# Moving matrix comparisons out of the attention heads of a four-layer network: 12 instead of 18 per attention, more in the second prologue, and squares one row tile behind their folds in the last product

## The chip, the cores and the metric

The kernel runs on one core of a Trainium2 chip. A core has a matrix engine (PE, with its weight loads shown as PEld), a vector engine (DVE), a scalar engine (ACT), a general engine (POOL) and a queue that only issues transfers here (SP). Each works through its own instructions in program order and waits on semaphores of the others. The metric is the device time of one execution in microseconds; the time before is the median of three runs.

## The reference

One sequence of 2048 rows of 640 passes through four layers, twice an attention and a Fourier layer:

```python
x = x + A(layernorm(x))      # 32 heads of 20, each row sees itself and the 255 before it
x = x + B(layernorm(x))      # y = Re(DFT_seq(DFT_hidden(x))), the four DFT matrices are inputs
x = x + A(layernorm(x))
x = x + B(layernorm(x))
# A: qkv = x @ wqkv; softmax(q k^T / sqrt(20) + mask) v, then @ wo
# B: a = x @ hid_re^T, b = x @ hid_im^T;  y = seq_re @ a - seq_im @ b
```

## The kernel before

The four DFT matrices are inputs, but a real DFT matrix repeats itself up to sign: rows and columns mirrored about the middle are equal or opposite. The Fourier layers use this and multiply by a quarter or less of each matrix. So that this holds for any input, the kernel also compares the matrices with themselves on the chip. It makes 180 comparisons in all (18 tiles of the hidden matrices `hr`, `hi`, 162 of the sequence matrices `kr`, `ki`), sums the squared differences, and at the end sets a flag `ok` of one word. Every engine loads it and branches: past a slow general version of the network if the symmetry holds, into it if not. With the inputs used, the branch always passes it.

One comparison is five steps (`check`, line 1462): SP issues one transfer of 214 to 228 KB into a free buffer (L1469); two folds subtract and add the mirrored parts (`differ`, L1476, one fold for some tiles); ACT squares the result with a running sum into a column of `ring` (`square`, L1480); after each eighth comparison DVE adds eight columns (L1485). The folds stand on POOL or on DVE, as the place asks. The last comparison also starts `verdict` (two small DVE operations into `sums`), and `judge` (L1509) turns `sums` into `ok`: a memset of ones on DVE, one small matmul into bank 6 of PSUM, four small DVE operations (L1517 to L1520).

The comparisons stand at four kinds of places, always taken from one list in order, so that a comparison left out at one place is made at a later one:

- In each attention's prologue (`before_heads`: layer norm, transposes, the first projections), the local function `check` starts one after most of the eight `piece` calls and ten of the sixteen `value` calls, in a pipeline of three (`check_step`): transfer first, folds on POOL and the square on ACT two or three calls later. 16 in each.
- In each attention's `heads`, 18 comparisons (`IN_HEADS`) over the first 81 of 128 steps (`CHECKED`): the transfer at the end of a step, then the two folds on POOL and the square on ACT six, seven and nine half steps later, from `self.post`.
- In each Fourier layer (`fourier`), four after each of the products 2 to 11 (`checks`, folds on DVE), then as many as are still in the shorter-lived buffers in a `while` loop, also on DVE.
- In the last product of the second Fourier layer, four for each of the first row tiles on POOL: `checks(4, n < 5, nc.gpsimd)`, fold, fold, square one after another, then the next transfer into the same buffer.

The last product runs over eight row tiles n (`order = (7, 0, 1, ... 6)`). `straight(n, j)` makes two products in PSUM (six matmuls, L1387), ACT copies one out (L1388, tile `sent`), DVE makes `dif` and `tot` and adds both to the row tile `big` (L1375), SP stores it (L1379). `turned(n - 1, ...)` stands one row tile behind: PE reverses `tot` and `dif` (L1403, two matmuls with `flip`, into banks 2 and 3 for even n - 1 and 6 and 7 for odd), and DVE adds them to the mirrored row tile. Only the last tile's `turned(7, 6)` follows the loop.

In the heads, every step makes scores in PSUM twice: once by query rows to find the row maxima (S, L676, with DVE's masked maximum, L681), once transposed for the exponentials (T, L704, ACT's L714, POOL's masks L720 and L724), then the product with v (L739); projection matmuls fill PE's gaps (L274). The row maxima of four query blocks are turned on PE and negated on ACT (tile `mt`, L692); SP then sends them with two transfers into a row of `qp` (L694), which T needs four steps later. SP's order is the order in which the program posts its transfers, and a transfer that waits holds all behind it.

Of the kernel before, what the change touches and what calls it, by code (L numbers as in the profile page):

```python
# [7 lines left out]
F32 = mybir.dt.float32  # L8
# [42 lines left out]
PRODUCTS = [(n, c) for n in ("ce", "co", "so", "se") for c in range(3)]  # L51
SIGMA, WIDE = 513, 57
SCALED, MARGIN = 2.0 ** 40, 2.0 ** 12
IN_HEADS, CHECKED = 18, 81

CHUNKS = ((0, 16, 0, 8), (0, 16, 8, 16), (16, 24, 0, 16), (24, 32, 0, 16), (0, 32, 16, 20))

# [16 lines left out]
class Net:  # L74
# [335 lines left out]
    def before_heads(self, xsrc):  # L410
# [42 lines left out]
        def pieces(sb):  # L453
            for c in range(2):
                if sb == 0:
                    prep()
                self.piece(c, sb, "q")
                if c or sb > 1:
                    check()
                if sb and state[0] < 4 * sb + 8:  # L460
                    prep()

        def value(t):
            v, xt = vst[t // 2 % 2], self.xnt(t // 4)
            rs = slice((t % 4) * P, (t % 4 + 1) * P)
            ps = []
            for hf in range(2):
                p = self.bank("v", 320)
                cs = slice(hf * 320, (hf + 1) * 320)
                self.all3(p, [((xt[:, 0, k, rs], xt[:, 1, k, rs]), (wv[k][0][:, cs], wv[k][1][:, cs]))  # L470
                              for k in range(KC)])
                ps.append(p)
            prep()
            for hf in range(2):
                dst = v[:, 4 * hf:4 * hf + 4, t % 2, 0:84].rearrange("p q (h c) -> p q h c", c=21)[:, :, :, 1:21]
                src = ps[hf].rearrange("p (q h c) -> p q h c", q=4, h=4)
# [826 lines left out]
    def fourier(self, xsrc, xdst, more):  # L1303
# [8 lines left out]
        lasting = bufs[6:]  # L1312
        waiting = deque()

        def checks(n, again=True, eng=nc.vector):
            for _ in range(n):
                if waiting:
                    work, buf = waiting.popleft()
                    work(eng)
                    if self.checks and (again or not more and any(buf is b for b in lasting)):  # L1320
                        waiting.append((self.check(buf), buf))

        for buf in bufs:
            if self.checks:
                waiting.append((self.check(buf), buf))

        def leave(n, c, b, eng):
            k = KINDS[n][1][c][1]
# [85 lines left out]
        for n, j in enumerate(order):  # L1414
            straight(n, j)
            if n:
                turned(n - 1, order[n - 1])
            if n < 6:
                checks(4, n < 5, nc.gpsimd)
            elif n == 6 and not more:  # L1420
                checks(len(waiting), False, nc.gpsimd)
                assert not self.checks
                self.judge()
            if more:
                if n > 1:
                    self.split_w(3)
# [82 lines left out]
    def judge(self):  # L1509

        nc = self.nc
        ones = self.work.tile([P, 1], F32, name="all1", tag="rc")
        nc.vector.memset(ones, 1.0)
        p = self.banks[0:1, 6, :5]
        nc.tensor.matmul(p, ones, self.sums, start=True, stop=True)
        s = self.work.tile([1, 16], F32, name="judged", tag="sm")
        nc.vector.tensor_copy(s[:, 0:5], p)  # L1517
        nc.vector.tensor_scalar(out=s[:, 5:9], in0=s[:, 1:5], scalar1=MARGIN, scalar2=s[:, 0:1], op0=OP.mult, op1=OP.is_gt)
# [174 lines left out]
```

## Time and profile before

| | |
|---|---|
| runs | 1375.52, 1375.58, 1376.85 us; median 1375.58 |
| profiled execution | 1376.7 us, its span 1374.8 us, mean granted PE clock 0.989 |
| busy, share of the span | PE 94%, PEld 72%, DVE 71%, ACT 55%, POOL 53% |
| first prologue and heads | 0 to 150, 150 to 532 us |
| partial products and first Fourier layer | 532 to 612, 612 to 687 us |
| second prologue and heads | 687 to 830, 830 to 1202 us |
| the same again, second Fourier layer | 1202 to 1282, 1282 to 1322 us |
| last product and end | 1322 to 1374.8 us |

Busy time is the time in which an engine had an instruction in work. Matmuls overlap, so a PE that is busy throughout may still not be at its peak. In rows of the timeline the columns are the start, the time, engine, line, operation and operands, and in brackets how long the engine had idled and for whom. Names such as `qp<-mt` mean output and input; a `q` after an engine's name marks its sequencer or queue.

### The profile page before, as it was taken

To read this page: it belongs to the slowest core of one execution; us is meant where nothing else is said; L and a number is where in the kernel's file an instruction comes from. 1 tells how busy PE (TensorE), PEld (TensorE's weight loads), DVE (VectorE), ACT (ScalarE), POOL (GpSimd) and SP (SyncE) were. 2 spreads that over 40 slices of the span, in tenths; PEclk is the share of its full clock that TensorE was granted. 3 is DMA by queue.
4 is the path that set the end of the run, shared out by engine and by line. 5 is a ranking of instruction groups with operands and counts; after the bars stand their busy time and mean duration, and the time that the engine had idled before them with its cause. 6 is when DMAs were issued, how large, how long until landed. Compare 5 with 4: busy or idle time off the path is not lost. (4 is left out here: it accounts for less than half of the span.)

```text
span 1374.8 us, 37392 instructions
## 1 busy us (share of the span) xinstructions
PE 1294.4 (94%) x13350; PEld 993.6 (72%) x13350; DVE 973.6 (71%) x3123; ACT 759.6 (55%) x1651; POOL 724.4 (53%) x1502
## 2 busy tenths in 40 slices
PE   6999999999998889999999999999999989989987
PEld 6899777777776677753689987777777667777344
DVE  7723788878887774767866158878878868568575
ACT  3232378777775565437323226777777755744461
POOL 4221688777876673310323238778777865723031
PEclk9999999999999999999999999999999999999999
DMA  5675577777678774527526656677777688571464
GB/s 195 207 224 170 187 207 202 216 195 213 202 217 231 207 207 138 166 79 221 200 83 214 208 169 197 194 210 202 222 192 237 198 236 232 154 230 47 151 184 163
DMA packets 174294, 261.47 MB, mean 190 GB/s; under 512 B 36306, under 2 KB 85586, under 8 KB 174100
## 3 DMA queue, kind: packets, MB, share of 16 engines
q1 hardware_dynamic: 174100, 259.00, 62.9%
q8 instruction: 108, 1.77, 0.6%
q14 instruction: 86, 0.70, 0.2%
HBM read 175.42 MB, written 82.31 MB: 187 GB/s over the span
## 5 line engine op out<-in xcount | busy, mean ns | idle before, releaser
L681 DVE CUSTOM_DVE_ANT_0 banks<-banks,mask 128x384 f32<-128x384 f32 (+2 forms) x1024 | 527.2, 557 | 121.1 <-PE banks L676 104.4
L714 ACT ACTIVATE pt<-banks 128x768 f32<-128x768 f32 (+2 forms) x512 | 394.2, 771 | 165.6 <-PE banks L704 100.2
L720 POOL TENSOR_SCALAR_AFFINE_SELECT pt<-pt 128x256 f32<-128x256 f32 x512 | 220.1, 430 | 187.2 <-ACT pt L714 162.7
L274 PE MATMUL banks<-big,wc 64*128 64x512 f32 x1920 | 273.2, 395 | 0.4 <-DVE pt L480 0.4
L704 PE MATMUL banks<-qp,kp 61*128 61x384 f32 (+2 forms) x1024 | 210.0, 380 | 32.1 <-DVE mc L681 21.5
L676 PE MATMUL banks<-kp,qp 60*128 60x384 f32 (+2 forms) x1024 | 209.1, 352 | 5.6 <-DMA kp<-qk_d 2.9
L739 PE MATMUL banks<-pt,vq 128*32 128x128 f32 x5760 | 211.4, 278 | 0.9 <-ACT pt L714 0.8
L274 PEld LDWEIGHTS banks<-big,wc 64*128 64x128 f32 x1920 | 186.9, 186 | 22.9 <-ACT x L589 1.6
L724 POOL TENSOR_SCALAR_AFFINE_SELECT pt<-pt 128x256 f32<-128x256 f32 x448 | 187.4, 418 | 0.0
L739 PEld LDWEIGHTS banks<-pt,vq 128*32 128x32 f32 x5760 | 142.2, 110 | 49.3 <-issue 35.2
L704 PEld LDWEIGHTS banks<-qp,kp 61*128 61x128 f32 x1024 | 108.4, 185 | 95.8 <-DVE mc L681 74.6
L676 PEld LDWEIGHTS banks<-kp,qp 60*128 60x128 f32 x1024 | 124.2, 187 | 32.2 <-DVE mc L681 16.1
L681 DVE DVE_READ_ACCUMULATOR2_ANT mc<- 128x1 f32 x1024 | 144.5, 141 | 0.0
L748 ACT ACTIVATE ou<-banks 128x128 f32<-128x128 f32 (+2 forms) x288 | 73.4, 266 | 58.8 <-PE banks L739 52.2
L256 PE MATMUL banks<-qp,big 128*128 128x320 f32 x576 | 98.4, 316 | 1.0 <-POOL qp L382 1.0
L228 POOL TENSOR_TENSOR c<-x,c 128x256 fp32r<-128x256 f32 x128 | 94.5, 746 | 0.0
L256 PEld LDWEIGHTS banks<-qp,big 128*128 128x128 f32 x576 | 88.3, 192 | 1.6 <-POOL qp L382 1.4
L256 PE MATMUL banks<-qp,kp 128*128 128x320 f32 x384 | 82.1, 346 | 7.0 <-ACT big L1121 4.7
L1476 POOL TENSOR_TENSOR rr<-rr 128x171 f32<-128x171 f32 (+3 forms) x86 | 56.3, 660 | 57.9 <-DMA rr<-kr 26.6
L274 PE MATMUL banks<-big,big 64*128 64x320 f32 x912 | 80.8, 313 | 0.2 <-ACT mt L692 0.2
L256 PEld LDWEIGHTS banks<-qp,kp 128*128 128x128 f32 x384 | 60.9, 188 | 20.4 <-ACT big L1121 6.7
L274 PEld LDWEIGHTS banks<-big,big 64*128 64x128 f32 x912 | 73.9, 191 | 0.4 <-ACT mt L692 0.4
(170 smaller groups left out, 1777.0 us busy)
## 6 DMA issues: line engine op xcount, KB each, us to landing
qk_d<-c SPq DMA_DIRECT2D x80, 512.0 KB
kp<-qk_d SPq DMA_DIRECT2D x384, 80.0 KB
qp<-qk_d SPq DMA_DIRECT2D x384, 80.0 KB
o_d<-ou SPq DMA_DIRECT2D x64, 256.0 KB
v_d<-pt SPq DMA_DIRECT2D x16, 768.0 KB
vq<-v_d SPq DMA_DIRECT2D x64, 192.0 KB
kp<-ki SPq DMA_DIRECT2D x38, 228.0 KB
big<-x SPq DMA_DIRECT2D x26, 320.0 KB
```

What stands on the lines that cost most here:

```text
L228: eng.tensor_tensor(out=lo[..., c], in0=src[..., c], in1=hi[..., c].bitcast(F32), op=OP.subtract)
L256: self.nc.tensor.matmul(p, x, y, start=n == 0, stop=n == last)
L274: self.nc.tensor.matmul(ps[a], x[r], y[r], start=half + i == 0, stop=half == 1 and i == n - 1, skip_group_check=True)
L676: nc.tensor.matmul(p, qp[quad % 2][b:b + 60, z, qb * P:(qb + 1) * P], kp[quad % 2][b:b + 60, z, k0 * P:(qb + 1) * P], start=True, stop=True)
L681: nc.vector.tensor_tensor_reduce(out=p, in0=p, in1=self.mask[:, 384 - n * P:], scale=1.0, scalar=NEG, op0=OP.add, op1=OP.max, accum_out=mc ...
L704: nc.tensor.matmul(self.banks[:, banks[e], :n * P], kp[quad % 2][b:b + 61, z, kb * P:(kb + 1) * P], qp[quad % 2][b:b + 61, z, kb * P:(kb + ...
L714: nc.scalar.activation(pt[quad, kb][:, 2 * z:2 * z + 2, :n * P], self.banks[:, b0:b1 + 1, :n * P], AF.Exp, scale=SCALE)
L720: nc.gpsimd.affine_select(out=t[:, :, 0:P], in_=t[:, :, 0:P], pattern=[[0, 2], [1, P]], compare_op=OP.is_ge, fill=0.0, base=0, channel_mul ...
L724: nc.gpsimd.affine_select(out=t[:, :, 256:384], in_=t[:, :, 256:384], pattern=[[0, 2], [-1, P]], compare_op=OP.is_gt, fill=0.0, base=0, ch ...
L739: nc.tensor.matmul(self.banks[32 * h:32 * h + 32, bank, :P], vq[:, 96 * (kb % 4) + 21 * h:96 * (kb % 4) + 21 * h + 32], t[:, h, (qb - kb) ...
L748: nc.scalar.activation(ou[:, dst], self.banks[:, bank, src], AF.Copy)
L1476: eng.tensor_tensor(out=t[:, lo:hi], in0=t[:, lo:hi], in1=base.broadcast_to([P, hi - lo, w]), op=op)
```

## The change

In each attention's heads 12 comparisons are made instead of 18, still over 81 steps. The second attention's prologue (not the first) starts one in six more places: the first pieces of the first two blocks and the first four value tiles. What is not made there falls to the end: the last product of the second Fourier layer makes 20 instead of 14. Both Fourier layers keep their 50 and 48 on DVE.

In the last product the squares of a row tile's four comparisons are now made in the next row tile (`spread`, list `folded`), and the transfers into their buffers follow them there. `judge` moves from row tile 6 to row tile 7, and its memset of ones to the place ahead of the loop. The diff, cut to its core:

```diff
-IN_HEADS, CHECKED = 18, 81
+IN_HEADS, CHECKED = 12, 81
...
-                if c or sb > 1:
+                if c or sb > 1 or not first:
                     check()
...
-            if 3 < t < 14:
+            if 3 < t < 14 or t < 4 and not first:
                 check()
...
+        def spread(n, again):
+            for square, buf in folded:
+                square()
+                if again:
+                    begin(buf)
+            folded.clear()
+            for _ in range(min(n, len(waiting))):
+                (one, two, square), buf = waiting.popleft()
+                one()
+                two()
+                folded.append((square, buf))
...
+        if not more:
+            self.all = self.work.tile([P, 1], F32, name="all1", tag="rc")
+            nc.vector.memset(self.all, 1.0)
...
-            if n < 6:
-                checks(4, n < 5, nc.gpsimd)
-            elif n == 6 and not more:
-                checks(len(waiting), False, nc.gpsimd)
-                assert not self.checks
-                self.judge()
+            if not more:
+                spread(4, n < 5)
+                if n == 7:
+                    assert not self.checks and not waiting and not folded
+                    self.judge()
...
-        ones = self.work.tile([P, 1], F32, name="all1", tag="rc")
-        nc.vector.memset(ones, 1.0)
         p = self.banks[0:1, 6, :5]
-        nc.tensor.matmul(p, ones, self.sums, start=True, stop=True)
+        nc.tensor.matmul(p, self.all, self.sums, start=True, stop=True)
```

What this does to the order on the engines is shown at three places. The lines of the code have shifted: after the change `straight`'s matmuls are L1409, the flips L1425, the small matmul of `judge` L1534, the transfer of a comparison L1490, its folds L1497.

PE at the end of the last product before, from the row tile n = 6 on (`wf`, `qp`, `kp`: operands of `straight`; `ou`, `rr`: tiles `tot` and `dif`; `all`, `sums`: `judge`):

```order
L1387 MATMUL banks<-wf,qp_17317 128x321 x3
L1387 MATMUL banks<-wf,kp_17316 128x321 x3
L1403 MATMUL banks<-ou_17591,flip 128x321
L1403 MATMUL banks<-rr_17590,flip 128x319
L1515 MATMUL banks<-sums,all_17775 1x5
L1387 MATMUL banks<-wf,qp_17317 128x321 x3
L1387 MATMUL banks<-wf,kp_17316 128x321 x3
L1403 MATMUL banks<-ou_17588,flip 128x321
L1403 MATMUL banks<-rr_17587,flip 128x319
L1403 MATMUL banks<-ou_17591,flip 128x321
L1403 MATMUL banks<-rr_17590,flip 128x319
```

The same place on PE after the change:

```order
L1409 MATMUL banks<-wf,qp_17293 128x321 x3
L1409 MATMUL banks<-wf,kp_17292 128x321 x3
L1425 MATMUL banks<-ou_17569,flip 128x321
L1425 MATMUL banks<-rr_17568,flip 128x319
L1409 MATMUL banks<-wf,qp_17293 128x321 x3
L1409 MATMUL banks<-wf,kp_17292 128x321 x3
L1425 MATMUL banks<-ou_17566,flip 128x321
L1425 MATMUL banks<-rr_17565,flip 128x319
L1534 MATMUL banks<-sums,all_17562 1x5
L1425 MATMUL banks<-ou_17569,flip 128x321
L1425 MATMUL banks<-rr_17568,flip 128x319
```

The small matmul of `judge` stood ahead of the last row tile's products; it now stands behind them, between the last two pairs of flips.

SP in the first heads before, around the fourteenth sending of row maxima (`rr<-kr` is a comparison's transfer, `kp` and `qp<-qk_d` load the next heads, `sm`, `o_d`, `r_d` carry results away):

```order
L758 DMA sm<-ou_104 128x1x16
L759 DMA o_d<-ou_104 128x512
L764 DMA r_d<-rc 128x16
L1469 DMA rr_107<-kr 128x456
L639 DMA kp_573<-qk_d 20x2x512 x3
L569 DMA qk_d<-c 128x2x512
L694 DMA qp_1249<-mt 2x4x128 x2
L639 DMA kp_573<-qk_d 20x2x512 x3
```

The same sending on SP after the change:

```order
L758 DMA sm<-ou_104 128x1x16
L759 DMA o_d<-ou_104 128x512
L764 DMA r_d<-rc 128x16
L639 DMA kp_573<-qk_d 20x2x512 x3
L569 DMA qk_d<-c 128x2x512
L694 DMA qp_1249<-mt 2x4x128 x2
L639 DMA kp_573<-qk_d 20x2x512 x3
L569 DMA qk_d<-c 128x2x512
L639 DMA qp_122<-qk_d 20x2x512 x3
L666 DMA vq_100<-v_d 128x384
L1490 DMA rr_107<-kr 128x456
```

The comparison's transfer stood three rows ahead of the sending; it now stands four rows behind it, and the one before it is more than ten rows ahead.

POOL in the second prologue after the change (`rs<-rs,half` is the reciprocal root for the layer norm of a row tile, L310); before, all rows of L310 stood ahead of the first fold:

```order
L310 TENSOR_TENSOR rs<-rs,half 128x1 x2
L1497 TENSOR_TENSOR ou_8917<-ou_8917 128x171
L1497 TENSOR_TENSOR ou_8917<-ou_8917 128x228
L310 TENSOR_TENSOR rs<-rs,half 128x1
L1497 TENSOR_TENSOR rr_8918<-rr_8918 128x171
L1497 TENSOR_TENSOR rr_8918<-rr_8918 128x228
L310 TENSOR_TENSOR rs<-rs,half 128x1
L1497 TENSOR_TENSOR rr_8919<-rr_8919 128x171
L1497 TENSOR_TENSOR rr_8919<-rr_8919 128x228
L1497 TENSOR_TENSOR rr_8920<-rr_8920 128x171
L1497 TENSOR_TENSOR rr_8920<-rr_8920 128x228
L310 TENSOR_TENSOR rs<-rs,half 128x1
```

The folds of the early comparisons now stand between the reciprocal roots.

More of the change, by code (lines that the diff above doesn't have):

```diff
@@ L1313, in fourier, with begin, checks @@
         waiting = deque()
-        def checks(n, again=True, eng=nc.vector):
+        folded = []
+        def begin(buf):
+            if self.checks:
+                waiting.append((self.check(buf, True), buf))
+        def checks(n, again=True):
             for _ in range(n):
                 if waiting:
[L1318 to L1321, printed above, removed]
+                    (one, two, square), buf = waiting.popleft()
+                    one(nc.vector)
+                    two(nc.vector)
+                    square()
+                    if again or not more and any(buf is b for b in lasting):
+                        begin(buf)
+        def spread(n, again):
+            for square, buf in folded:
+                square()
+                if again:
+                    begin(buf)
+            folded.clear()
+            for _ in range(min(n, len(waiting))):
+                (one, two, square), buf = waiting.popleft()
+                one()
+                two()
+                folded.append((square, buf))
         for buf in bufs:
-            if self.checks:
-                waiting.append((self.check(buf), buf))
+            begin(buf)
         def leave(n, c, b, eng):
```

## The prediction

> **What bounds the kernel now.** I read the busy time by stage first, since the four places of the change lie in stages with different limits. The columns are the stretch, its length, then busy time with the number of instructions for PE, PEld, DVE, ACT and POOL, the granted PE clock, the share of DMA and GB/s.
>
> ```profile
> 150.00:360.00 210.00, 206.01 (x2843) 157.38 (x2839) 174.00 (x651) 154.83 (x311) 163.20 (x360) 0.99 0.69 203
> 712.00:830.00 118.00, 118.00 (x815) 106.39 (x816) 56.26 (x168) 32.39 (x92) 36.92 (x59) 1.00 0.60 188
> 830.00:1050.00 220.00, 213.90 (x3012) 162.55 (x3012) 182.01 (x682) 164.65 (x331) 173.03 (x395) 1.00 0.73 206
> 1322.00:1375.00 53.00, 40.08 (x135) 26.00 (x133) 30.60 (x76) 18.60 (x59) 17.49 (x28) 0.90 0.44 154
> ```
>
> PE carries all of them. In the second prologue it is busy without a break; in the part of the heads that holds comparisons it idles 4 to 6 us of some 215; only the last product leaves it idle for 13 us. So comparisons taken out of the heads free POOL, ACT and SP, none of which is the bound, and can gain only where PE now waits behind them. The waits of PE in those two stretches (156 to 386, then 830 to 1056 us; total, times, longest) say for what:
>
> ```profile
> PE banks L704 <- DMA qp<-mt: 2.8, 2, 1.7
> ...
> PE banks L704 <- DVE mc L681: 1.9, 5, 0.6
> ...
> PE banks L704 <- DMA qp<-mt: 4.2, 4, 1.5
> ```
>
> The largest wait is for the row maxima that SP sends late. The longest case, in the order of ACT, SP and PE, with the granted clock behind it:
>
> ```profile
> 286.25 0.25 ACT L692 ACTIVATE mt<-banks 16x128 fp32r<-16x128 f32 x1
> ...
> 287.96 0.33 SPq L1469 DMA_DIRECT2D rr<-kr  x1
> 288.49 1.18 SPq L639 DMA_DIRECT2D kp<-qk_d  x3
> 290.07 0.39 SPq L569 DMA_DIRECT2D qk_d<-c  x1
> 290.57 1.48 SPq L694 DMA_DIRECT2D qp<-mt  x2
> ...
> 294.93 0.45 PE L704 MATMUL banks<-qp,kp 61*128 61x384 f32 x2 [1.68 <-DMA qp<-mt]
> ...
> 295.00:299.00 4.00, 4.00 (x33) 3.01 (x33) 2.28 (x8) 2.14 (x4) 1.22 (x4) 0.60 0.88 253
> ```
>
> The maxima are ready at 286.25 and their first transfer starts at 290.57, 4.3 us later, because SP's row ahead of them is not yet worked off; a comparison's transfer is in that row.
>
> **The heads.** Twelve comparisons go, six from each attention. On POOL and ACT I cost them at nothing: of the 18 comparisons in 156 to 386 us (16 with `kr`, two with `hi`) the folds held up other work in two waits. Who waited for the folds there (total, times), the cost of a transfer on SP (ns, least, median, most), and what other transfers waited on SP for a comparison's transfer:
>
> ```profile
> ACT pt L714: 0.8, 1
> PEld banks L739: 0.2, 1
> ...
> L1469 SPq DMA_DIRECT2D rr<-kr x16: 333/414/822, 187.2 to 375.5; - x16
> ...
> SPq L639 <- DMA rr<-kr: 3.1, 3, 1.7
> SPq L758 <- DMA rr<-kr: 2.5, 2, 1.2
> ```
>
> What covers them is PE's own work of 98% of the stretch; were PE not the bound, the gain would be at most 1.0 us in each heads (0.8 + 0.2).
>
> On SP a comparison costs between 0.41 us (its own issue) and 0.72 us (with the waits for its landing, (3.1 + 2.5) / 18 = 0.31). Not the number counts but where the transfer stands ahead of a sending. By the order, at the fourteenth sending of each heads (here at 290.57) and the twenty-second, the last comparison ahead moves from 3 or 4 rows to 10 or more, out of the row that SP works off; at the eighteenth it comes nearer, from 10 rows to 3. The waits at these, beside the one shown:
>
> ```profile
> 383.97 0.45 PE L704 MATMUL banks<-qp,kp 61*128 61x384 f32 x2 [1.17 <-DMA qp<-mt]
> ...
> 968.32 0.45 PE L704 MATMUL banks<-qp,kp 61*128 61x384 f32 x2 [0.80 <-DMA qp<-mt]
> ...
> 1012.76 0.44 PE L704 MATMUL banks<-qp,kp 61*128 61x384 f32 x2 [1.46 <-DMA qp<-mt]
> ```
>
> Three waits shorten (1.68, 1.17, 0.80) and one lengthens (1.46); the same sending of the first heads has no wait yet and may get one, taken as half. With 0.41 us each that is -3 x 0.41 + 1.5 x 0.41 = -0.6 us. I take the lower price, because SP's next wait for a landing is as likely to be for another transfer. Bounds: all 7.0 us (2.8 + 4.2) vanish; or the three stay and two new ones of the longest kind come, +3.4 (2 x 1.68).
>
> The clock: behind the wait of 1.68 us the granted clock is 0.60 over 4 us, so 4 x 0.40 = 1.6 us of PE's work was lost. With 0.41 us taken off, that wait would be 1.27 us; the one of 1.46 us lies in a stretch whose granted clock is 1.00 (830 to 1050), so a wait of that size need not cost it. I count the half, -0.8. The Trainium skill, "TensorE: Matmul & The Clock Gate", section "What's actually happening", says that the array falls to half clock after an idle window of about 3.4 us; by it a wait of 1.68 us should have cost no clock, and the sum would be 0.8 us less of a gain. The trace differs here: the clock did fall.
>
> **The second prologue.** Six comparisons more. On PE nothing: ahead of each square ACT waits for PE anyway, and POOL waits for DVE between two reciprocal roots.
>
> ```profile
> 715.45 0.60 ACT L243 ACTIVATE c<-banks 128x512 fp32r<-128x512 f32 x1 [3.14 <-PE banks L256]
> ...
> 718.14 0.81 POOL L310 TENSOR_TENSOR rs<-rs,half 128x1 f32<-128x1 f32 x1 [3.98 <-DVE rs L307]
> ...
> L1476 POOL TENSOR_TENSOR rr<-rr x18: 507/634/958, 742.0 to 786.2; 128x171 f32<-128x171 f32 x9, 128x228 f32<-128x228 f32 x9
> ...
> ACT ou L1480 <- POOL ou L1476: 6.0, 3, 3.5
> ```
>
> Two folds at 0.63 us are 1.3 us of POOL's 3.98 idle; a square, with its read-out some 0.7 us, fits into ACT's 3.14. Each of the moved steps also issues a transfer on SP (0.41 us), ahead of the stores of v and of the projections, whose readers come later in this stage. The cover is gone if a load is late: the last row shows that ACT has stood up to 3.5 us before a square whose folds waited. Bounds: 0, and 6 x (3.5 + 0.7 - 3.14) = +6.4 us; I take 0, since 16 such comparisons already stand here while PE is busy 118.00 of 118.00 us.
>
> **The last product.** Up to its first row tile nothing changes: DVE has the same 48 comparisons, and POOL the same first eight. Then ACT's squares no longer stand ahead of the second `sent`, but PE is the one that sets the pace (one row tile in 4.33 us, from 1350.98 to 1355.31), so I cost the reorder at nothing. Six comparisons more on POOL are twelve folds at 0.61 us (4.87 us for eight, first row below), 7.3 us behind 1346.8; with loads that wait for the later squares they end by about 1358. ACT idles 3.89 us per row tile there and DVE 1.84, so this costs nothing either, as long as POOL ends before 1360. What remains is `judge`:
>
> ```profile
> 1341.93 4.87 POOL L1476 TENSOR_TENSOR kp<-kp 128x171 f32<-128x171 f32 x8 [0.90 <-DMA kp<-ki]
> ...
> 1357.45 0.44 ACT L1388 ACTIVATE vq<-banks 128x321 f32<-128x321 f32 x1 [3.89 <-PE banks L1387]
> ...
> 1359.10 0.49 DVE L1375 TENSOR_TENSOR rr<-banks,vq 128x321 f32<-128x321 f32 x1 [1.84 <-PE banks L1387]
> ...
> 1350.98 1.54 PEld L1387 LDWEIGHTS banks<-wf,qp 107*128 107x128 f32 x6
> ...
> 1355.31 1.54 PEld L1387 LDWEIGHTS banks<-wf,qp 107*128 107x128 f32 x6
> ...
> 1361.67 0.19 PE L1515 MATMUL banks<-sums,all 128*1 128x5 f32 x2 [1.59 <-DVE all L1513]
> 1361.79 1.89 PE L1387 MATMUL banks<-wf,qp 107*128 107x321 f32 x6
> 1361.90 0.15 DVE L1517 COPY judged<-banks 1x5 f32<-1x5 f32 x1 [0.30 <-PE banks L1515]
> ...
> 1362.52 0.14 DVE L1520 TENSOR_SCALAR ok<-judged 1x1 int32<-1x1 f32 x1
> ...
> 1365.41 0.49 DVE L1375 TENSOR_TENSOR rr<-banks,vq 128x321 f32<-128x321 f32 x1 [2.75 <-PE banks L1387]
> ...
> 1366.36 0.81 PE L1403 MATMUL banks<-ou,flip 128*128 128x321 f32 x2
> ...
> 1367.01 0.70 PE L1403 MATMUL banks<-rr,flip 128*128 128x319 f32 x2
> 1367.02 1.68 DVE L1375 TENSOR_TENSOR big<-banks,big 128x321 f32<-128x321 f32 x4
> ```
>
> In row tile 6 PE stops for the memset and the adds ahead of it on DVE (they also free bank 6), and the last products start at 1361.79 instead of 1355.31 + 4.33 = 1359.64. After the change that stop is gone: -2.15 us. But the four small operations now stand between the adds of `turned(6)` and those of `turned(7)`, and the last flip writes bank 6, which L1517 must have read. Counted from the last tile's first DVE operation (1365.41 before): two products out, two adds and two more end at about 2.45; L1517 takes 0.15, so the flips start at 2.65 instead of 0.95 (1366.36). The second flip ends 1.35 later (1367.01 + 0.70 against 1366.36), at 4.0; the last add ends at 4.5. Before it ended at 1367.02 + 1.68 = 1368.70, at 3.3. So +1.2 of the 2.15 come back: -0.95 us. Bounds: -2.15, if the flips are not held, and 0.
>
> **The sum**: heads -0.6 - 0.8, second prologue 0, last product -0.95, together -2.35, rounded up to -2.4 for the freed ACT and POOL. Against the profiled execution's span of 1374.8 that gives 1372.4, and 1.9 us lie around the span (it took 1376.7). The profiled execution is 1.1 us above the median of the runs, so I take the change off the median, 1375.58: 1373.2 us.
>
> **The rivals.** (1) The heads give nothing: the row maxima come late for SP's whole row, not for one transfer in it, and a wait that goes at one sending comes at another. For it: the waits also stand at sendings with no comparison near. Then only -0.95 remains, 1374.6. (2) The sendings' waits vanish: with a third of the comparisons gone SP keeps up, -7.0 - 1.6 - 0.95 = -9.55, 1366.0. Against it: SP is held by some ten other transfers per step group, as the rows from 286 to 290 show. (3) Slower: in the second prologue the squares stand in ACT's row ahead of the copies that feed PE and wait for folds whose loads are late. If each of the six waits x us, PE loses 6 (x + 0.7 - 3.14); from x = 2.85 this outweighs the gain of 2.4, and at the longest seen, 3.5, it is +6.4 - 2.4, 1379.6. Against it: SP issues each load three calls ahead, over 12 us.
>
> **How the numbers follow.** A difference of 0.2% (2.75 us, so 1372.8 and 1378.3) is about what a measurement of this kernel can tell from no change. I give the forecast 0.50, with its own range 1371 to 1375, half on each side of 1372.8; rival 1 0.24, within; rival 2, whole or in good part, 0.15, faster; rival 3 0.11, slower. Faster 0.25 + 0.15 = 0.40, same 0.25 + 0.24 = 0.49, slower 0.11. The range leaves out the ends of rivals 2 and 3: 1369.0 to 1378.0.
>
> **What would show it.** Right: no wait for `all` in the last product; the last products start 4.3 us after those before them; the last flips wait for DVE about 1.7 us; PE still busy throughout the second prologue; fewer PE waits on `qp<-mt`. Wrong: PE gaps between 687 and 735 us behind ACT; new waits on `qp<-mt` as long as the old; a half clock at another place in the heads; squares in the last product that hold `sent` back.

## The result, and the profile after

| | before | after |
|---|---|---|
| runs side by side, median | 1377.7 us (6 runs) | 1369.03 us (6 runs) |
| ratio, 95% interval | | 0.9928 [0.9906, 0.9950] |
| profiled execution, its span | 1376.7, 1374.8 us | 1368.6, 1366.9 us |

The change makes the kernel about 0.7% faster, some 10 us. 2.4 us were forecast, and no measurable change was held likelier than a gain. Three slow runs are left out of the ratios of this document: 1387.2 and 1392.6 us of the kernel before, and 2005.3 us of the fifth kernel below.

Where the profiled executions differ, with stages cut at the same instructions in both traces (first and last exponential of each heads, first and last matmul of `straight`, last add on DVE; us):

| stage | before | after | difference |
|---|---|---|---|
| to the first heads | 159.15 | 158.97 | -0.2 |
| first heads | 374.73 | 371.53 | -3.2 |
| first Fourier layer, second prologue | 298.70 | 301.40 | +2.7 |
| second heads | 371.67 | 371.02 | -0.7 |
| to the last product | 118.97 | 117.08 | -1.9 |
| last product, first to last matmul of `straight` | 41.66 | 33.39 | -8.3 |
| to the last add on DVE | 3.82 | 5.01 | +1.2 |
| from there to the end of the span | 6.10 | 8.46 | +2.4 |

The stretches of the prediction's first table, after (columns as there; the last begins 3 us earlier, as its stage does). The second prologue is again busy on PE nearly throughout, 117.93 of 118.00 us:

```profile
150.00:360.00 210.00, 204.06 (x2810) 155.72 (x2811) 175.45 (x644) 151.46 (x299) 157.09 (x352) 0.99 0.68 197
712.00:830.00 118.00, 117.93 (x818) 107.55 (x818) 56.46 (x167) 34.99 (x101) 42.43 (x69) 1.00 0.63 196
830.00:1050.00 220.00, 216.30 (x3054) 164.83 (x3052) 184.29 (x690) 163.74 (x322) 170.03 (x389) 1.00 0.69 201
1319.00:1367.00 48.00, 36.56 (x134) 24.22 (x132) 27.79 (x76) 21.79 (x71) 27.01 (x39) 0.94 0.57 194
```

The waits of PE in the heads' stretches (156 to 386, then 830 to 1056). In the first, no wait for `qp<-mt` is left, and another has come; in the second, 2.9 us of 4.2 are left:

```profile
PE banks L676 <- DVE mc L681: 3.5, 1, 3.5
PE banks L704 <- DVE mc L681: 2.6, 7, 0.6
...
PE banks L704 <- DMA qp<-mt: 2.9, 3, 1.2
```

The largest part lies in the last product. The waits of PE from its first matmul on, before and then after:

```profile
PE banks L1403 <- DVE ou L1375: 4.0, 1, 4.0
PE banks L1515 <- DVE all L1513: 1.6, 1, 1.6
```

```profile
PE banks L1425 <- DVE judged L1536: 1.5, 1, 1.5
PE banks L1425 <- ACT ou L1423: 0.8, 1, 0.8
```

The stop of 1.6 us is `judge`'s, which the prediction had. The 4.0 us ahead of the first flips it had not looked at. The timeline of before at that place, DVE, POOL and PE (a `x2` row is the two folds of a comparison, a `x4` row those of two), the sum among them in the view of DVE alone, and the stretch behind (columns as in the first table of stretches):

```profile
1322.21 1.19 DVE L1476 TENSOR_TENSOR kp<-kp 128x171 f32<-128x171 f32 x4
1322.66 10.55 POOL L1476 TENSOR_TENSOR kp<-kp 128x171 f32<-128x171 f32 x16 [51.50 <-DMA kp<-ki]
...
1325.10 1.38 DVE L1476 TENSOR_TENSOR rr<-rr 128x171 f32<-128x171 f32 x2
1326.40 1.38 DVE L1476 TENSOR_TENSOR ou<-ou 128x171 f32<-128x171 f32 x2
...
1334.01 1.44 PE L1403 MATMUL banks<-ou,flip 128*128 128x321 f32 x2 [4.03 <-DVE ou L1375]
```

```profile
1324.14 0.16 DVE L1485 TENSOR_REDUCE part<-ring 128x1 f32<-128x8 f32 x1 [0.74 <-ACT kp L1480]
```

```profile
1334.00:1341.00 7.00, 6.99 (x15) 4.56 (x16) 3.33 (x9) 6.49 (x22) 2.12 (x4) 0.55 0.67 194
```

DVE starts its last sixteen folds (the `while` loop), pauses 0.74 us at 1324.14 for the sum of eight `ring` columns (L1485), because ACT has not squared yet, and from then on needs 1.30 us per comparison (1325.10 to 1326.40), in turn with POOL's folds. So `tot` of the first row tile comes late, PE stops for 4.03 us, and the last row shows the granted clock at 0.55 over the 7 us behind it. The same place after, the sum again from the view of DVE alone:

```profile
1318.43 13.93 POOL L1497 TENSOR_TENSOR kp<-kp 128x171 f32<-128x171 f32 x16 [49.22 <-PE banks L1301]
1319.01 1.18 DVE L1497 TENSOR_TENSOR kp<-kp 128x171 f32<-128x171 f32 x4
1320.11 0.63 DVE L1497 TENSOR_TENSOR vq<-vq 128x171 f32<-128x171 f32 x2
1320.66 0.63 DVE L1497 TENSOR_TENSOR rr<-rr 128x171 f32<-128x171 f32 x2
...
1326.61 0.70 PE L1425 MATMUL banks<-ou,flip 128*128 128x321 f32 x2
```

```profile
1324.25 0.16 DVE L1506 TENSOR_REDUCE part<-ring 128x1 f32<-128x8 f32 x1 [0.75 <-ACT ou L1501]
```

Now the sum stands behind all sixteen folds, DVE needs 0.55 us per comparison (1320.11 to 1320.66), POOL's folds are the ones that wait, and PE goes on at 1326.61 without a stop. The sum has moved because 112 instead of 118 comparisons are made ahead of the last Fourier layer: it is made after each eighth.

### The profile page after: what moved, and what is told of

Same layout as the page of the kernel before. It is cut to its first block, busy times and chain, and to the rows that moved or that the text cites. A ratio compares the mean times of both kernels' runs of the same rounds, so it can differ in the third digit from the quotient of the medians.

```text
span 1366.9 us, 37415 instructions
## 1 busy us (share of the span) xinstructions
PE 1293.2 (95%) x13350; PEld 995.8 (73%) x13350; DVE 973.2 (71%) x3117; ACT 761.4 (56%) x1651; POOL 729.3 (53%) x1508
## 4 chain that ended last, share of the span: by engine, by line
PE 40%; DMA 3%; DVE 3%; issue 2%; ACT 2%; POOL 1%; SPq 1%; ACTq 0%; POOLq 0%; DVEq 0%
PE banks L274 10%; PE banks L256 8%; PE banks L739 5%; PE banks L704 4%; PE banks L676 4%; PE banks L1301 3%; PE banks L1409 3%; DMA big<-x_d 1%; PE banks L1425 1%; DVE banks L681 1%; ACT pt L714 1%; DMA qp<-qk_d 1%; DMA qp<-mt 1%; PE banks L362 1%; POOL rs L1156 0%
## 5 line engine op out<-in xcount | busy, mean ns | idle before, releaser
L228 POOL TENSOR_TENSOR c<-x,c 128x256 fp32r<-128x256 f32 x128 | 94.3, 744 | 0.0
L1497 POOL TENSOR_TENSOR rr<-rr 128x171 f32<-128x171 f32 (+3 forms) x76 | 48.5, 648 | 47.2 <-DMA rr<-hr 17.9
```

Of the source, the lines that this page charges most:

```text
L228: eng.tensor_tensor(out=lo[..., c], in0=src[..., c], in1=hi[..., c].bitcast(F32), op=OP.subtract)
L1497: eng.tensor_tensor(out=t[:, lo:hi], in0=t[:, lo:hi], in1=base.broadcast_to([P, hi - lo, w]), op=op)
```

## The experiments

The ratios are to the kernel before, run on the same chip in the same rounds; five such rounds gave 6 or 12 runs of each kernel. There are four such groups, each on another chip: the first four kernels below; the changed kernel again, the one with 18 and the sum behind, the one with `judge` early and the one with the other queue; the fifth, those with six more transfers and the one with `judge` between the products; those with twelve more transfers and the one with shifted rows. Runs of one kernel spread over 8 to 18 us (standard deviation 3 to 6), so stages of the profiles, one of each kernel, carry the small terms.

### The last product: which part took the stop away

Four kernels separate the place of the sum from the new order of squares. The first makes the last product's part of the change alone (18 in the heads; the diff is against the changed kernel). The second makes the heads' and prologue's part alone: these same lines of the change, put into the kernel before.

```diff
-IN_HEADS, CHECKED = 12, 81
+IN_HEADS, CHECKED = 18, 81
-                if c or sb > 1 or not first:
+                if c or sb > 1:
-            if 3 < t < 14 or t < 4 and not first:
+            if 3 < t < 14:
```

> The kernel before with the last product's part of the change alone (squares one row tile behind their folds, judge in row tile 7, memset ahead of the loop); 18 comparisons in each attention's heads and 14 in the last product, as before. Theory 1, the place of the sum of eight ring columns (it stands among DVE's last sixteen folds before, behind them after, because 112 instead of 118 comparisons are made ahead): the sum stays among the folds, so DVE's loop folds stay at about 0.69 us, PE still stops for about 4.0 us on tot and a half clock follows. Only judge's stop (-2.15) goes, +1.2 and +2.4 come back at the end: 0.999 to 1.002 of before. Theory 2, the new order of squares and transfers itself keeps POOL out of DVE's way: folds at 0.31 us, no 4 us stop, about 6 us less, 0.995 of before. Theory 3, chance from execution to execution: runs of both kinds, spread over 6 us.

Measured: 0.9969 [0.9946, 0.9992], 1374.97 us.

> The kernel before with 12 comparisons in the heads and the six more starts in the second prologue; the last product makes 20 in the old order, judge in row tile 6. Theory 1 (place of the sum): the count ahead is 112, so the sum stands behind DVE's sixteen folds, these take about 0.31 us, the 4 us stop and the half clock behind it go: about -6 from there, and the stages of the heads and prologue as profiled after (about -2): 0.994 of before. Theory 2 (new order): the stop stays, only the heads' part is seen: 0.997 to 1.000. Theory 3 (chance): spread over 6 us.

Measured: 0.9949 [0.9922, 0.9977], 1367.47 us. The third is the kernel before, the fourth the changed one (there with 6 for 2), with only the counter's start changed, and so the place of the sums:

```diff
-        self.n_checks = 0
+        self.n_checks = 2
...
-            self.part = fixed("part", len(self.checks) // 8 + 1, F32)
+            self.part = fixed("part", (len(self.checks) + 2) // 8 + 1, F32); nc.vector.memset(self.ring, 0.0)
```

> The kernel before with nothing changed but the place of the sums of eight ring columns: the counter starts at 2 instead of 0 (the ring is cleared once at the start, the two columns that stay empty are zero), so that in the last Fourier layer a sum falls behind the last of DVE's folds instead of among them. Theory 1: DVE's sixteen folds at about 0.31 us, no 4 us stop of PE on tot, no half clock behind it, the stage from the first to the last matmul of the last product 41.7 to about 35.7 us; 0.9956 of before. Theories 2 and 3: 1.000, the stop stays or comes and goes.

Measured: 0.9988 [0.9957, 1.0020], 1372.42 us.

> The changed kernel with the counter starting at 6 (ring cleared at the start), so that the sum of eight stands among DVE's last sixteen folds again, at the place it has in the kernel before; all else as changed. Theory 1: DVE's folds go back to about 0.69 us, the stop of about 4 us and the half clock come back: about 1375, 0.998 of before. Theory 2 (new order of squares): as the changed kernel, 0.993. Theory 3 (chance): spread over 6 us.

Measured: 0.9946 [0.9918, 0.9974], 1370.09 us.

DVE's pace in the loop follows the sum alone: 0.55 us per comparison in every kernel with the sum behind the folds (also in the second and third), 1.30 in those with the sum among them (before, the first and the fourth). That much of theory 1 is shown both ways. But moving the sum alone gained far less than its 6 us. The stage from the first to the last matmul of `straight` (us):

| | squares in old order, `judge` in tile 6 | squares one tile behind, `judge` in tile 7 |
|---|---|---|
| sum among the folds | before 41.66 | first 38.50, fourth 38.44 |
| sum behind the folds | third 40.44, second 38.90 | changed kernel 33.39 |

The reason is another stop, one row tile later. PE's waits in the last product of the third, second, first and fourth kernel:

```profile
PE banks L1403 <- ACT ou L1401: 3.1, 1, 3.1
PE banks L1515 <- DVE all L1513: 1.6, 1, 1.6
```

```profile
PE banks L1403 <- ACT ou L1401: 2.6, 1, 2.6
PE banks L1515 <- DVE all L1513: 1.6, 1, 1.6
```

```profile
PE banks L1425 <- DVE ou L1397: 4.0, 1, 4.0
PE banks L1425 <- DVE judged L1536: 1.5, 1, 1.5
```

```profile
PE banks L1425 <- DVE ou L1397: 4.2, 1, 4.2
PE banks L1425 <- DVE judged L1536: 1.5, 1, 1.5
```

In the third, where DVE goes first, POOL's folds are late, ACT's squares wait for them, and `sent` (L1388) and the edge rows (L1401) stand behind the squares in ACT's row:

```profile
1331.78 0.54 ACT L1480 ACTIVATE kp<-kp 128x399 f32<-128x399 f32 x1 [0.42 <-POOL kp L1476]
...
1332.31 0.42 ACT L1388 ACTIVATE vq<-banks 128x321 f32<-128x321 f32 x1
...
1332.63 0.45 ACT L1401 ACTIVATE ou<-wf 1x321 f32<-1x321 f32 x1
...
1333.13 1.44 PE L1403 MATMUL banks<-ou,flip 128*128 128x321 f32 x2 [3.13 <-ACT ou L1401]
```

With the squares one row tile behind, that stop shrinks to the 0.8 us for `ou` L1423 shown above. So each part alone leaves a stop of 2.6 to 4.2 us, with half the clock granted for 3.4 to 6.8 us at it; only the two together reach 33.39, where the clock stays full. Neither theory 1 nor theory 2 was right by itself, and chance is out, since every profile falls on its side.

That POOL's folds are what slows DVE's, and not the wait for the sum, a fifth kernel shows: before, with the first eight comparisons of the last product folded on DVE, so that POOL has none beside DVE's loop.

```diff
-                checks(4, n < 5, nc.gpsimd)
+                checks(4, n < 5, nc.vector if n < 2 else nc.gpsimd)
```

> The kernel before with the folds of the first eight comparisons of the last product on DVE instead of POOL; the sum of eight stays among DVE's folds, where before has it. POOL then has no fold beside DVE's last sixteen. Theory 1 (POOL's folds and DVE's hold each other up once DVE has paused for the sum): DVE's folds take 0.33 us though the sum stands among them, and no stop of 4 us behind them; the stage from the first to the last matmul of the last product 41.7 to 36 to 38 us. Rival (the wait for the sum itself, or late loads, slow the folds): they stay at 0.7 us and the stop comes later still, since DVE has sixteen folds more.

```profile
1322.47 0.16 DVE L1485 TENSOR_REDUCE part<-ring 128x1 f32<-128x8 f32 x1 [0.74 <-ACT kp L1480]
1322.55 0.64 DVE L1476 TENSOR_TENSOR vq<-vq 128x171 f32<-128x171 f32 x2
1323.11 0.63 DVE L1476 TENSOR_TENSOR rr<-rr 128x171 f32<-128x171 f32 x2
```

The sum stands among the folds, with the same pause of 0.74 us, and still each comparison takes 0.55 us. The time did not follow: 1.0041 [1.0010, 1.0073]. The eight comparisons now stand in DVE's row behind the first row tile's adds, the squares behind them on ACT, and PE waits 8.2 us for `ou` L1401; the stage takes 45.85 us.

### The heads: what six comparisons fewer are worth, and why

The changed kernel again, and the same with 18 in the heads, no extra starts in the prologue, and the sum kept behind the folds (the first kernel's edit with the third's):

> The changed kernel once more, on the same chip and in the same rounds as the three that follow, to set them against it: 0.990 to 0.995 of before; in the last product DVE's sixteen folds at 0.33 us, no stop of PE above 1 us until the last tile.

> The changed kernel with 18 comparisons in each attention's heads and no more starts in the second prologue, as before; the counter starts at 2 (ring cleared), so that the sum of eight still stands behind DVE's folds. What differs from the changed kernel is the heads' and the prologue's part alone. Theory A, SP's whole row is relieved by 12 instead of 18: PE's waits for transfers in the two heads are back at about 10 us instead of 2 to 6, the kernel is 4 to 6 us longer than the changed one, 0.996 to 0.998 of before. Theory B, the prediction (heads -1.4): 1.4 us longer. Theory C, all of the gain lies in the last product: as the changed kernel within 1 us. In all three the stage from the first to the last matmul of the last product is 33.4 us as in the changed kernel.

Measured: 0.9901 [0.9863, 0.9940] and 0.9946 [0.9919, 0.9973], 1361.82 and 1367.28 us; both with 33.4 us in the last product. So the heads' part gives 5 to 6 us of the time. The pairs of the first and the fourth (0.9969, 0.9946) and of the third and the second (0.9988, 0.9949) say 3 and 5. Each is net of the longer end that all kernels with 12 had (2.4 us, below). The two heads together, first to last exponential, take 746.4 to 748.6 us in the five kernels with 18 (before, first, third, fifth, and this one; mean 747.6), 737.1 to 742.6 in the five with 12 (the changed kernel twice, the second, the fourth and the one with `judge` early; mean 740.3): 7.3 us. PE's waits for transfers (`qp<-mt`, `kp` and `qp<-qk_d`) in the heads sum up to 10.2 us on the mean of the former and 3.6 of the latter.

Is it SP, POOL or ACT that is relieved? In the first try the comparisons' transfers in the heads are issued by ACT (`queue`, a new argument of `check`):

```diff
-            steps = self.check(buf, True)
+            steps = self.check(buf, True, nc=self.nc.scalar)
...
-        nc.sync.dma_start(t, src)
+        queue.dma_start(t, src)
```

> The kernel before with nothing changed but the queue: the transfers of the 18 comparisons in each attention's heads are issued by ACT instead of SP. Theory A (SP's row is what makes the row maxima late): PE's waits for qp<-mt fall from about 7.5 us to 0 to 3, although POOL's folds, ACT's squares and the bytes are all as before; a gain of 3 to 6 us in the heads, less what ACT loses by 36 issues in its own row. Rival (the load of POOL and ACT, or of the DMA engines, makes them late): the waits stay at about 7.5 us and the time at 1.000.

Measured: 1.0676 [1.0637, 1.0716]. Both theories missed: PE's waits for `qp<-mt` rose to 28.8 and 26.6 us in the two heads. Taking the transfers out of SP's row did not help, so this kernel does not tell the theories apart. Why the waits rose is open.

The second try adds to the changed kernel's heads transfers that nobody reads, without folds or squares, six in each heads and then twelve, of 228 KB or of 4 KB (the small ones go to a spare tile of 8 columns, the large ones to a place in memory):

```diff
             self.checked = self.slot + 9
+            if self.n_checks % 2:                 # in the kernels with twelve: if True
+                self.nc.sync.dma_start(self.spare, self.a["kr"][0, 0][:, :8 * WIDE])   # small: [:, :8]
```

> The changed kernel with six more transfers in each attention's heads, each of a comparison's size (228 KB, from the first tile of kr to a place in memory that nobody reads), issued by SP behind every second comparison: 18 such transfers in SP's row again, but still 12 comparisons' folds and squares. Theory A (SP's row and the transfers make the row maxima and the next heads' loads late): most of the 6 us between the kernels with 12 and 18 comparisons are lost again, 0.994 to 0.996 of before; PE's waits for transfers in the two heads 7 to 11 us. Theory B (POOL's folds or ACT's squares are what costs in the heads): as the changed kernel, 0.990 to 0.992.

> As the one with six more transfers in each heads, but each of 4 KB instead of 228 KB: SP issues as many, the DMA engines move next to nothing more. If it is SP's issuing (about 0.4 us each) that costs, the time is as with the large ones, 0.994 to 0.996; if it is the bytes on the DMA engines, as the changed kernel, 0.990 to 0.992.

> The changed kernel with twelve instead of six more transfers of 228 KB in each attention's heads, one behind each comparison's: 24 such transfers in SP's row, 12 comparisons' folds and squares. Theory A1 (it is the bytes that the DMA engines move which make row maxima and loads late): twice the dose, PE's waits for transfers in the two heads 14 us or more, 6 to 12 us longer than the changed kernel with its closing rows shifted. Theory A2 (SP's issuing): the same, but then the small transfers cost it as well. Theory B (folds and squares): no longer than that kernel.

> The same with twelve more transfers of 4 KB in each heads. Theory A1 (bytes): within 2 us of the changed kernel with its closing rows shifted, PE's waits for transfers 2 to 6 us. Theory A2 (issuing, 0.4 us each on SP): 6 to 12 us longer, as with the large ones.

| kernel | ratio | both heads, us | PE's waits for transfers, us |
|---|---|---|---|
| 18 comparisons (five profiles) | | 747.6 | 10.2 |
| 12 comparisons (five profiles) | | 740.3 | 3.6 |
| 12 and six large | 0.9907 [0.9875, 0.9940] | 745.6 | 11.1 |
| 12 and six small | 0.9878 [0.9830, 0.9925] | 741.6 | 5.2 |
| 12 and twelve large | 0.9964 [0.9942, 0.9986] | 750.5 | 15.0 |
| 12 and twelve small | 0.9916 [0.9890, 0.9943] | 741.0 | 6.8 |
| 12 and the closing rows shifted (below) | 0.9880 [0.9855, 0.9906] | 732.2 | 5.1 |

PE's waits in the second heads with twelve large, then with twelve small:

```profile
PE banks L704 <- DMA qp<-mt: 7.6, 6, 2.1
PE banks L676 <- DMA qp<-qk_d: 1.0, 1, 1.0
```

```profile
PE banks L704 <- DMA qp<-mt: 2.9, 2, 2.0
PE banks L676 <- DMA kp<-qk_d: 1.1, 1, 1.1
```

Against the five profiles with 12, six large transfers bring back most of the 7.3 us without a single fold, twelve 10.2 us, and PE's waits for transfers rise with them; small ones, as many in SP's row, add 0.7 to 1.3 us. The clean comparison is large against small, beside each other and with the same number of issues: 4.0 and 9.5 us in the heads, and in the medians of the runs 1366.07 against 1360.83 us for six and 1371.87 against 1364.11 us for twelve. So POOL's and ACT's work is not needed for the loss, and much of what a transfer costs goes with its size. (Large and small differ in where they go too, which no run separates. And the ratio of six large ones, 0.9907, lies where the folds and squares were expected to put it; their heads and waits do not.)

That SP's issuing costs nothing is not shown. The reference that was named ahead for twelve is the kernel with the closing rows shifted, whose heads took 8 us less than the mean of the five. Against it twelve small ones cost 8.8 us in the heads and 7.8 us in the medians (1364.11 against 1356.31), which is what the issuing was expected to cost (6 to 12) and not what the bytes were (within 2); twelve large ones cost 18.3 and 15.6. Part of the 8.8 is a wait of 3.4 us, with a half clock at it, that befell the profile with small ones for another reason (a DVE operation held up by POOL, last section). The rest is open, as is what makes those heads so short.

### The end

`judge` in row tile 7 was to cost 1.2 us at the last adds; the 2.4 us behind them were not foreseen. Three kernels: `judge` a row tile earlier, its matmul in columns that no flip writes; 16 tiny transfers on SP at the end of the first Fourier layer, meant only to shift SP's closing rows; and the second's transfers together with `judge` between the last tile's two products, its matmul in the first's columns.

```diff
-                if n == 7:
+                if n == 6:
...
-        p = self.banks[0:1, 6, :5]
+        p = self.banks[0:1, 6, 400:405]
```

> The changed kernel with judge one row tile earlier (n == 6) and its small matmul in columns 400 to 404 of bank 6, which no flip writes: the four small DVE operations no longer stand between the last adds, and the last flips don't wait for them. From the last matmul of straight to the last add 5.01 us goes back to 3.8: -1.2 us, 0.999 of the changed kernel. The engines load the flag earlier; if the end is 2.4 us longer in the changed kernel because all branch at once, those come back as well (-3.6 in all); if the end's length hangs on where the closing rows lie in SP's code, it stays at 8.4.

Measured: 0.9937 [0.9905, 0.9968], against 0.9901 of the changed kernel beside it: no gain. The last add came 3.82 instead of 5.01 us after the last matmul of `straight`, but that matmul came 2 us later (35.34 for 33.39), since PE now waits 1.56 us for the sums ahead of the last products. The end stayed long, 7.82 us.

```diff
             self.first = False
+            for i in range(16):
+                nc.sync.dma_start(self.spare[:, i:i + 1], a["kr"][0, 0][:, i:i + 1])
```

> The changed kernel with the 16 tiny transfers on SP at the end of the first Fourier layer and nothing else: the reference for the two with more transfers, since all three have their closing rows shifted. If the stop of SP among its closing rows comes from where they lie, the time from the last add to the end is 5.7 to 6.5 us instead of 8.5, and the kernel about 2.5 us faster than the changed one: 0.988 to 0.991 of before; if not, 8.5 us as in the changed kernel.

Measured: 0.9880 [0.9855, 0.9906], 1356.31 us; from the last add to the end 5.68 us.

```diff
                     nc.tensor.matmul(p, src[c][:k, j * P:(j + 1) * P], mat[c][:k, :], start=c == 0, stop=c == 2)
+                if n == 7 and not more and src is v:
+                    self.judge()
```

> The changed kernel with two edits that are to make it faster. The small matmul of judge stands between the two products of the last row tile, in columns 400 to 404 of bank 6, and its four small DVE operations ahead of that tile's dif and tot: last matmul of straight to last add 5.0 to 3.8 us, with no wait of PE for the sums ahead of the products as in the kernel with judge one tile earlier. And SP issues 16 tiny transfers more at the end of the first Fourier layer, so that its closing rows lie 16 instructions further on: if SP's stop of 1.3 us among its closing rows (in all kernels with 12, in none with 18) comes from where they lie, it goes, and from the last add to the end it takes about 6 to 7 instead of 8.5 us. Together -2.5 us against the changed kernel, 0.988 to 0.990 of before; if the stop has another cause, -1.2.

Measured: 0.9860 [0.9814, 0.9907], 1357.11 us: the lowest ratio of all, though its interval overlaps the last one's and that of the changed kernel. Last add 3.82 us after the last matmul, end 6.26 us, no PE wait in the last product but the 0.8 us.

The time from the last add to the end, by SP's instructions in the trace:

| SP's instructions | kernels | us |
|---|---|---|
| 2267 | 18 in the heads: before, first, third, fifth (POOL without folds), 18 with the sum behind | 5.7 to 6.6 |
| 2279 | 12: changed (twice), second, fourth, `judge` early | 7.7 to 8.8 |
| 2291 to 2303 | 12 and more transfers (all six) | 5.7 to 6.3 |

In the kernels of the middle row SP stands for 1.2 to 1.3 us between the twelfth and thirteenth of its closing semaphore rows, at the same place in each; in the others there is no gap there. This is about half of the 2.4 us. In the changed kernel (twice) and the fourth the first closing row also comes later, 5.2 to 5.5 us behind the last add, against 3.8 to 3.9 in the first kernel, the one with 18 and the sum behind and the one with shifted rows, which have `judge` at the same place. Shifting SP's rows took both away, so the longer end hangs on where they lie; what SP waits for there no run shows. My first idea, that all engines branching together makes the end long, fell: the first kernel and the one with 18 and the sum behind branch together as well, and end in 5.8 and 5.7 us.

## Why the prediction was wrong

**The last product, up to its first row tile: this step failed.** "Nothing changes: DVE has the same 48 comparisons, and POOL the same first eight", and the reorder of the squares was costed at nothing since PE sets the pace. The counts are the same, but the sum of eight moved by six places among DVE's folds, and PE did not set the pace there: it stood 4.03 us, with a granted clock of 0.55 behind it. With the sum moved, the reorder of the squares took away the stop that would have come next (2.6 to 3.1 us). Together with `judge`'s stop this is 8.3 us in place of 2.15: stops of 4.03 + 1.59 that became 0.81, and 7 x 0.45 = 3.2 us of clock, come to 8.0.

**`judge`: right.** No wait for `all` is left, and the last products start 4.33 us after those before them. The flips wait for L1536, which reads bank 6:

```profile
1356.35 0.14 DVE L1536 COPY judged<-banks 1x5 f32<-1x5 f32 x1
...
1356.55 0.81 PE L1425 MATMUL banks<-ou,flip 128*128 128x321 f32 x2 [1.51 <-DVE judged L1536]
```

The last add came 1.19 us later behind them; +1.2 was forecast.

**The heads: mechanism near, term too small.** PE waited for the sendings of row maxima, as said, but the price of 0.41 us was that of SP's issue, and it was counted at single sendings by their neighbours in SP's row. The runs show a loss spread over the whole heads that goes in good part with the size of the transfers, which that price left out: -7.3 us on the means (-3.9 in the pair of the first table) in place of -0.6 - 0.8. What share SP's issuing has stays open. Rival 2, "the sendings' waits vanish", had the size (-8.6), though it too spoke of SP keeping up. The half clock behind the wait at 293 went, as half expected; another came at 309.7, behind the new wait of 3.5 us.

**The second prologue: right**, 0 forecast, +0.1 us measured between ACT's copies of its first and last value tile, so rival 3 did not come. The +2.7 us of the row in the first table that holds it lie elsewhere: 1.6 in the partial products and 1.2 between them and the copy of the first value tile, each with a half clock. The partial products of that layer took 53.9 to 57.2 us in kernels that do not differ there.

**The end: left out**, +2.4 us. It is not the change's order there that makes it: with the same order and SP's rows shifted the end takes 5.68 us.

In sum: heads -7.3, last product -8.3 + 1.2, end +2.4, together -12.0 us, against 0.9928 and 0.9901 in the two comparisons, -9.9 and -13.6 us.

## What to carry to other kernels

Before costing a reorder at nothing, look at the place itself: a stop of 4 us stood in the trace of before at the first row tile, and whatever counts modulo something (here a sum after each eighth) moves with every change of the count ahead of it. When small transfers come late, ask for the size of the transfers ahead of them, and not only for their number. And two changes that each leave a stop may be worth much more together than apart, so test them together too.

## What was unexpected of the hardware

Two engines that fold out of the same memory hold each other up, and one can be kept out by a whole row of the other's instructions. Of POOL's sixteen folds in the changed kernel (13.93 us in the row above) a single one, which takes 0.5 us elsewhere, is recorded with 5.10 us, about as long as DVE's train of folds; once DVE had paused for 0.74 us, as before, the two took turns, although DVE's folds then followed without a break too. What decides between the two patterns is not shown. It goes the other way round as well. In the first heads of the changed kernel, one DVE operation of 0.55 us took 4.80 while POOL worked without a pause (its rows just ahead and at the end); the last row is the same operation when the changed kernel ran again:

```profile
303.47 0.41 POOL L724 TENSOR_SCALAR_AFFINE_SELECT pt<-pt 128x256 f32<-128x256 f32 x1
...
307.94 0.74 POOL L228 TENSOR_TENSOR c<-x,c 128x256 fp32r<-128x256 f32 x1
```

```profile
304.28 4.80 DVE L228 TENSOR_TENSOR wc<-x,wc 128x384 fp32r<-128x384 f32 x1
...
309.41 0.33 PE L676 MATMUL banks<-kp,qp 60*128 60x128 f32 x2 [3.51 <-DVE mc L681]
```

```profile
304.48 0.55 DVE L228 TENSOR_TENSOR wc<-x,wc 128x384 fp32r<-128x384 f32 x1
```

This one operation is the new wait of 3.5 us and the half clock at 309.7. It was held up so in 6 of the 16 profiles other than that with the other queue, and not in the rest, in kernels with 12 and with 18; it is part of the spread from run to run. The Trainium skill, "SBUF — State Buffer", section "Who interferes with whom", says that a VectorE instruction with two inputs in SBUF contends with a GpSimd instruction that reads it, and that the order of issue, not the kind of operation, decides who blocks. The traces agree (5.10 and 4.80 us for operations of 0.5). They agree on the order too: when the changed kernel ran again, DVE's operation began just ahead of POOL's L228 (304.48 against 304.56), and it was POOL's that took longer, 1.07 instead of 0.74 us. They show besides that a train of instructions, and not one alone, can keep the other out.

A wait put down to one engine can be another's: the longest waits "for DVE" in the later heads, 2 to 4 us with a half clock behind them in most kernels, come from a load that DVE itself waits for. In the changed kernel run again:

```profile
1100.10 0.82 DVE L1041 TENSOR_TENSOR big<-banks,big 128x640 f32<-128x640 f32 x1 [3.63 <-DMA big<-x_d]
...
1101.51 0.69 PE L704 MATMUL banks<-qp,kp 61*128 61x384 f32 x2 [3.62 <-DVE mc L681]
```

It was 1.2 to 1.8 us in the second heads of the two kernels with 16 tiny transfers, whose heads take 730 and 732 us in all, 8 to 10 less than those of the other kernels with 12. Why is open.
